# A gated attention and MLP kernel: the softmax shift from the first 512 keys, a half chunk of x loaded later, one split on GpSimd

## The chip, the core and the metric

The kernel runs on one core of a Trainium2 chip. The metric is the device time of one execution in microseconds (us). The core has five engines with a queue of instructions each, worked off in order: PE (matrix products, results in PSUM), DVE (vector), ACT (scalar functions, exponentials), POOL (GpSimd) and SP, which here only issues DMAs. Engines wait for each other by semaphores.

## The reference

One layer: `x` is 2048 x 512. Attention has 32 heads of 16 and one shared key and value head; beside it runs an MLP of width 1792 with squared ReLU; a gate per row mixes the two.

```python
g = sigmoid((x * gate_w).sum(-1, keepdims=True))
q = (x @ wq).reshape(B, S, 32, 16).transpose(0, 2, 1, 3)
k, v = x @ wk, x @ wv
p = softmax(einsum("bhqd,bkd->bhqk", q, k) * 16 ** -0.5)
a = einsum("bhqk,bkd->bhqd", p, v).transpose(...).reshape(B, S, 512) @ wo
b = maximum(x @ w1 + b1, 0) ** 2 @ w2 + b2
return g * a + (1 - g) * b
```

## The kernel before

Products in fp32 are made of rounded parts: each operand is split into `r` (rounded to a faster format) and `l` (the rest), and `r*r + r*l + l*r` is summed. So `xr`, `xl` stand for x, `wqr`, `wql` for wq, `qr`, `ql` for q; making a pair takes one cast and one subtraction.

The softmax uses no row maximum. Its shift is a bound: the norm of the query times the greatest norm of a key. The score product itself applies it: `qa` holds the rows of q and one row with the query norms (`nrm`), and `k_aug` holds the rows of k and one row with minus the greatest key norm (`km`), written by `k_shift`. A score group S is the product of 128 keys with 2 x 2 blocks of queries; ACT takes its exponential into a tile `e`; the context product (`acc<-e,v_ext`) sums `e` with v. At the end sums outside a safe range would send the kernel to an exact branch; this does not happen with these inputs.

The front, before the first score: x comes in four chunks of 512 rows, each in two DMAs of 512 KB (`x_load`; tiles `xf` for chunks 0 and 1, `xk` for 2 and 3), wq in four blocks (`wq_load`, tiles `wqf`). `kv_sums` makes k and v of one chunk, `kv_copy` copies them to SBUF (`kvc`), `k_rows` spreads k over the rows that `k_aug` needs, `k_round` (ACT) and `k_parts` (DVE) put it there. `kv_gather`, `kv_keep` and `kv_turn` turn k and v so that keys stand on partitions: for the key norms (`k_squares`, then the maximum) and for `v_ext`. `q_early` makes the first block of q, `qnorm` its norms, `q_direct` brings them into `qa` by SP's and POOL's DMA queues.

After that the work is interleaved. A span is one unit of other work (a block of q, of the MLP, of a projection): a number of matrix products M into one PSUM bank named `mm`, of which there are two, so the third unit takes the bank of the first. A phase is one text such as `"S0 M K M S1 ..."`: S is a score group, M a product of the unit, `02` and `12` the two halves of a score group that DVE copies from a third bank (`x`) into `e`, and K in the first phase a step left over from the front. While the program is written out, a planner keeps the estimated times of PE, ACT and DVE and places DVE's and ACT's other work by a list (`soon`: the span from which an entry may go, its cost, the work), in its order: the first entry has to go before the second is looked at. `wq_round` rounds a block of wq on ACT, `wq_rest` subtracts on DVE. When a unit of q is done, DVE casts its bank into `qr` and forms `ql` and the squares; with that the bank is free.

Nothing reorders instructions on the chip: the order on each engine is the order in which the program writes them out.

Of the kernel before, what the change touches and what calls it, by code (L numbers as in the profile page):

```python
# [58 lines left out]
    (4, 4, SECOND): ("02 S0 M M S1 M 12 M S3", (0, 1, 3, 2)),  # L59
    (4, 3, WHOLE): ("M 02 S0 M S1 12 M S3", (0, 1, 3, 2)),  # L60
}
FIRST_PHASE = "S0 M K M S1 M M M 02 M S3 M M M S4 M 12 M M S5", (0, 1, 3, 4, 5, 2)
HC = CH // 2

Q_ROWS = (0, 0, DH), (DH, 0, DH), (RS + 1, 1, DH), (RS, 2, 1)
FRONT_A, FRONT_V = 8, 22
LAST_OK = NC * KT - 1
FULL = 128 * LW * NC * KT

# [104 lines left out]
def mix_kernel(ctx: ExitStack, tc: tile.TileContext, xT, xs, gw, wkv, wq, wo, w12, b1, b2, cst, out):  # L174
# [67 lines left out]
    with fast, tc.tile_pool(name="at", bufs=1) as at, \  # L242
# [8 lines left out]
        def aside():  # L251
            return mp.tile([128, CH], F32, name="x", bufs=1)
# [8 lines left out]
        nc.scalar.dma_start(wkvf, wkv)  # L261
        xf, xw = {}, {}

        def x_load(c):

            for a in range(2):
                xw[c, a] = (at.tile([128, 2, CH], F32, name="xf", tag="e", bufs=10) if c < 2 else
                            at.tile([128, 2, CH], F32, name="xk", tag="w2p", bufs=5))
                nc.sync.dma_start(xw[c, a], xT[c, a])  # L269
            for k in range(KT):  # L270
                xf[c, k] = xw[c, k // 2][:, k % 2]

        def wq_load(t, n):
            nc.sync.dma_start(wqp[t // 2][:, t % 2:t % 2 + n], wq[t:t + n].rearrange("t p m -> p t m"))
# [1 line left out]
        x_load(0)  # L276
        wq_load(0, 1)
        nc.sync.dma_start(cs, cst)
        for c in range(1, NC):
            x_load(c)  # L280
        wq_load(1, 1)
        nc.gpsimd.dma_start(b1t, b1)
        gwb = at.tile([128, D], F32, name="gwb", tag="lc", bufs=2)

        blk = at.tile([128, 32], BF, name="blk")
        ones = at.tile([96, 128], BF, name="ones")
        kmx = at.tile([128, NK], F32, name="kmx")
        kmt = at.tile([128, 1], F32, name="kmt")
        km = at.tile([128, 1], F32, name="km")
        z = at.tile([128, NS], F32, name="z")  # L290
# [5 lines left out]
        for i in range(FRONT_V):  # L296
# [1 line left out]


        ks = {}  # L300
        rows_of = {0: lambda: two[:, 0], 1: lambda: late_kv[:, 1], 2: aside,
                   3: lambda: mp.tile([128, CH], F32, name="mm")}
        kvt = [at.tile([128, 2, CH], F32, name="kvc", tag="e", bufs=10) for _ in range(2)]
        kvc = [t[:, i] for t in kvt for i in range(2)]
        kvq, kb = {}, {}
# [1 line left out]
        def kv_sums(c, parts=range(KT)):  # L307

            if parts[0] == 0:
                kvq[c] = late_kv[:, 0] if c == 3 else aside() if c == 1 else mp.tile([128, CH], F32, name="mm")  # L310
            for k in parts:
                nc.tensor.matmul(kvq[c][32 * k:32 * k + 32], wkvf[:, k], xf[c, k], start=True, stop=True,
                                 skip_group_check=True, tile_position=(0, 32 * k))

        def kv_copy(c):
            nc.scalar.activation(kvc[c], kvq[c], AF.Copy)
# [19 lines left out]
                else:  # L336
                    nc.vector.tensor_scalar(row, src, -1.0, None, op0=OP.mult)  # L337

        ks2 = []
        kvg, gathered = [], {}  # L340

        def kv_gather(c):

            gathered[c] = mp.tile([128, CH], F32, name="mm") if c % 2 else aside()
            for j in range(4):
                nc.tensor.matmul(gathered[c][32 * j:32 * j + 32, :128], cs[:, C_SEL:C_SEL + 2 * DH],
                                 kvc[c][:, j * 128:(j + 1) * 128], start=True, stop=True,
                                 skip_group_check=True, tile_position=(0, 32 * j))

        def kv_keep(c):  # L350
            if not kvg:
                kvg.append(of_tile("kvg", F32))
            nc.scalar.activation(kvg[0][:, c * 128:(c + 1) * 128], gathered[c][:, :128], AF.Copy)

        def kv_turn(c):
            nc.tensor.transpose(acc[:, c * 128:(c + 1) * 128], kvg[0][:, c * 128:(c + 1) * 128], ident)

        def k_squares(i, n):
            if not ks2:
                ks2.append(of_tile("ksq", F32)[:, :NK * DH].rearrange("p (i d) -> p i d", i=NK))  # L360
            ksq = ks2[0]
            k = kvp[:, i:i + n, :DH]
            nc.scalar.activation(ksq[:, i:i + n], k, AF.Square)
            nc.vector.tensor_reduce(kmx[:, i:i + n], ksq[:, i:i + n], AX.X, OP.add)

        def k_max():
            nc.vector.tensor_reduce(kmt, kmx, AX.X, OP.max)
            pn = mp.tile([128, CH], F32, name="mm")
            nc.tensor.matmul(pn[:, :128], kmt.to_broadcast([128, 128]), ident, start=True, stop=True)

            def rest():
                nc.vector.tensor_reduce(km, pn[:, :128], AX.X, OP.max)
                nc.vector.tensor_scalar(km.bitcast(I32), km.bitcast(I32), 0.5, ROOT, op0=OP.mult, op1=OP.add)

            return rest

        def v_rows():
            nc.vector.tensor_copy(v_ext[:, :, 0:32:2], kvp[:, :, DH:])
# [11 lines left out]
        def of_tile(name, dt=F32R):  # L390
            return at.tile([128, CH], dt, name=name, tag="of", bufs=10)
# [8 lines left out]
        def q_early():  # L400
            q = mp.tile([128, CH], F32, name="mm")
            mm(q, q_terms(0, 0))
            qr, ql = of_tile("qr"), of_tile("ql")

            def rest():
                nc.vector.tensor_tensor(ql, q, qr.bitcast(F32), OP.subtract)
                nc.vector.tensor_tensor(sq8[:, 0], qr.bitcast(F32), qr.bitcast(F32), OP.mult)

            return qr, ql, (lambda: nc.scalar.activation(qr, q, AF.Copy)), rest

# [25 lines left out]
        def qnorm(tiles, p8=None):  # L436

            if p8 is None:
                p8 = aside()
            n = 32 * len(tiles)  # L440
            for i, (it, sq) in enumerate(tiles):
                nc.tensor.matmul(p8[32 * i:32 * i + 32], blk, sq, start=True, stop=True, tile_position=(0, 32 * i))  # L442
            nrm, tmp = of_tile("nrm"), of_tile("tmp", F32)
            root(nrm[:n], p8[:n], tmp[:n])
            if tiles[0][0] == 0:
                q_direct(RS, nrm, 1, (nc.sync, nc.gpsimd))
            for i, (it, sq) in enumerate(tiles):
                nc.sync.dma_start(qs[2][it:it + 2].rearrange("u r d a n -> (u r d a) n"),
                                  nrm[32 * i:32 * i + 8].bitcast(F32))
                done.update((it, it + 1))  # L450
# [110 lines left out]
        def wq_round(t):  # L561
            nc.scalar.activation(wqr[:, t], wqf[t], AF.Copy)
# [35 lines left out]
        wq_round(0)  # L598
        wq_rest(0)
        kv_copy(0)  # L600
        nc.vector.tensor_copy(blk, cs[:, C_BLK:C_BLK + 32])
        qr, ql, q_round, q_rest = q_early()
        x_pair(1, 0)
        kv_sums(1)
        two = sp.tile([128, 2, CH], F32, name="s")
        k_rows(0)
        nc.scalar.activation(xr[1][:, 2:], xw[1, 1], AF.Copy)  # L607
        q_round()
        q_rest()
        q_direct(0, qr, DH, (nc.sync, nc.gpsimd))  # L610
        q_direct(DH, qr, DH, (nc.sync, nc.gpsimd))
        q_direct(RS + 1, ql, DH, (nc.sync, nc.gpsimd))
        wq_load(2, 2)
        kv_copy(1)
        kv_gather(0)
        k_round(0)
        kv_keep(0)
        k_parts(0)
        kv_sums(2)
        qnorm([(0, sq8[:, 0])], mp.tile([128, CH], F32, name="mm"))  # L620
        kv_copy(2)
        acc = ap.tile([128, CH], F32, name="acc")
        kvp = acc.rearrange("p (i d) -> p i d", i=NK)
        kv_turn(0)
        kv_gather(1)
        kv_keep(1)
        kv_gather(2)
        kv_keep(2)
        nc.vector.tensor_tensor(xl[1][:, 2:], xw[1, 1], xr[1][:, 2:].bitcast(F32), OP.subtract)
        late_kv = sp.tile([128, 2, CH], F32, name="s")  # L630
        kv_sums(3)
        kv_copy(3)
        kv_turn(1)
        kv_turn(2)
        k_squares(0, 12)
        kv_gather(3)
        kv_keep(3)
        kv_turn(3)
        k_squares(12, 4)
        wq_round(1)  # L640
        k_rows(1)
        norm = k_max()
        nc.vector.tensor_copy(wqr[:, 2], wqf[2])
        k_rows(2)
        k_round(1)
        norm()
        k_shift(0, True)
        k_parts(1)
        k_round(2)
        k_parts(2)  # L650
        wq_rest(1)
        q_write(0, 0, qr, ql, nc.sync)

        def last_rows():

# [5 lines left out]
            act(0.6)  # L661
            dve(0.75)

        held, begun = 0.0, [0]
        chores, divisions = [], []
        soon = [(1, 0.7, lambda: wq_rest(2)), (1, 0.9, lambda: k_shift(1)), (1, 0.4, v_rows),
                (1, 0.7, lambda: (act(0.64), wq_round(3), wq_rest(3))), (2, 0.9, lambda: k_shift(2)), (3, 0.9, lambda: k_shift(3)),
                (3, 0.0, lambda: gates())]
        soon += [(6, 1.2, lambda k=k: x_split(2, k)) for k in range(KT)]
# [628 lines left out]
        def phase(slots, n, m):  # L1298
# [23 lines left out]
            for i in range(len(rows[0])):  # L1322
                for r in range(2):
                    item = rows[r][i]
                    if item == "M":
                        span.product(r)
                    elif item == "K":
                        if r == 0:
                            last_rows()
                    elif item[0] == "S":  # L1330
                        score_part(scored + int(item[1:]), r)
                    else:
                        score_copy(scored + int(item[1:]), r)
                    exps(todo)
                at_pe += PAIR
# [164 lines left out]
```

## Time and profile before

| | before |
|---|---|
| median of 3 runs | 1173.19 us (1172.84 to 1173.22) |
| profiled execution | 1173.13 us |
| its span | 1171.6 us |
| PE busy | 1163.5 us (99%) |
| ACT busy | 1022.9 us (87%) |
| DVE busy | 687.2 us (59%) |
| POOL busy | 67.9 us (6%) |
| granted PE clock | 1.0 |

The profile is one execution. Its rows give the start and the length of an instruction in us, the engine, the line, what it writes and reads, and in brackets how long its engine sat idle before it and what ended that. `x8` counts instructions in a row; one fp32 product is two matmuls there, so four products are `x8`. A q behind an engine's name (`SPq`) is the queue that issues DMAs.

### The profile page before, as it was taken

How to read it: one execution, taken by the hardware profiler on the slowest of the kernel's cores; microseconds unless marked ns; L12 is line 12 of the kernel's file. 1: busy time of each engine (PE TensorE's matmuls, PEld its weight loads, DVE VectorE, ACT ScalarE, POOL GpSimd, SP SyncE). 2: the span in 40 equal slices, each digit the busy share in tenths (PEclk: the TensorE clock that was granted, in tenths of full speed). 3: DMA queues.
4: the chain of work that ended last, by engine and by line, in shares of the span. 5: the costliest groups of instructions: out<-in, count | busy, mean ns of one | idle time of the engine just before them, and what ended most of it. 6: DMA issues, size and time to landing. Idle time of an engine off the chain costs nothing.

```text
span 1171.6 us, 31973 instructions
## 1 busy us (share of the span) xinstructions
PE 1163.5 (99%) x13793; PEld 779.6 (67%) x13793; DVE 687.2 (59%) x1174; ACT 1022.9 (87%) x1143; POOL 67.9 (6%) x125
## 2 busy tenths in 40 slices
PE   8999999999999999999999999999999999999998
PEld 4666666676766666666666666666666666666665
DVE  6877886764754745553666636535556537534554
ACT  7789999999988888888888898989888888888885
POOL 1000111010100000100000000001000000001000
PEclk9999999999999999999999999999999999999999
DMA  7245535251533513320434305224215224222101
GB/s 265 98 157 174 185 110 199 92 195 48 174 121 119 181 39 119 110 83 20 145 110 141 97 20 176 98 66 154 65 47 168 79 66 133 95 75 92 56 38 39
DMA packets 49290, 130.26 MB, mean 111 GB/s; under 512 B 11350, under 2 KB 11846, under 8 KB 48632
## 3 DMA queue, kind: packets, MB, share of 16 engines
q1 hardware_dynamic: 37272, 90.68, 24.1%
q0 software_dynamic: 11728, 37.43, 8.8%
q8 instruction: 109, 1.79, 0.6%
q14 instruction: 37, 0.30, 0.1%
q10 hardware_dynamic: 144, 0.07, 0.0%
HBM read 87.92 MB, written 35.64 MB: 105 GB/s over the span
## 4 chain that ended last, share of the span: by engine, by line
PE 97%; DMA 1%; ACT 1%; SPq 0%; DVE 0%; issue 0%
PE acc L964 39%; PE mm L1271 34%; PE s L907 19%; PE x L907 5%; DMA xf<-in_xT 1%; DMA wqf<-in_wq 0%; ACT e L944 0%; DVE ot L1231 0%; SPq L414 0%; PE s L213 0%; SPq L269 0%; ACT xr L607 0%; PE mm L321 0%; PE x L1053 0%; PE x L442 0%
## 5 line engine op out<-in xcount | busy, mean ns | idle before, releaser
L944 ACT ACTIVATE e<-s 128x1024 f32<-128x1024 f32 x765 | 748.1, 1024 | 102.5 <-PE s L907 99.4
L928 DVE COPY e<-x 128x512 f32<-128x512 f32 x518 | 358.4, 692 | 444.8 <-PE x L907 276.0
L964 PE MATMUL acc<-e,v_ext 128*32 128x256 f32 x8192 | 470.2, 381 | 0.0
L907 PE MATMUL s<-qa,k_aug 49*128 49x512 f32 x1530 | 407.4, 410 | 0.5 <-DVE k_aug L337 0.3
L964 PEld LDWEIGHTS acc<-e,v_ext 128*32 128x32 f32 x8192 | 252.5, 110 | 192.7 <-issue 40.4
L944 ACT ACTIVATE e<-e 128x1024 f32<-128x1024 f32 x259 | 272.8, 1056 | 0.2 <-ACT e L944 0.2
L907 PEld LDWEIGHTS s<-qa,k_aug 49*128 49x128 f32 x1530 | 214.7, 185 | 85.4 <-ACT e L944 38.6
L1271 PE MATMUL mm<-w2p,hr 64*128 64x512 f32 x1128 | 242.2, 392 | 0.0
L907 PE MATMUL x<-qa,k_aug 49*128 49x512 f32 x518 | 213.7, 413 | 0.0
L1271 PEld LDWEIGHTS mm<-w2p,hr 64*128 64x128 f32 x1128 | 160.8, 186 | 18.8
L1271 PE MATMUL mm<-xragain,w1p 64*128 64x512 f32 x448 | 119.7, 392 | 0.0
L907 PEld LDWEIGHTS x<-qa,k_aug 49*128 49x128 f32 x518 | 95.3, 184 | 36.1 <-DVE e L928 19.1
L1271 PE MATMUL mm<-xr,w1p 64*128 64x512 f32 x448 | 114.7, 392 | 0.0
L1271 PEld LDWEIGHTS mm<-xragain,w1p 64*128 64x128 f32 x448 | 70.0, 186 | 6.9
L1271 PEld LDWEIGHTS mm<-xr,w1p 64*128 64x128 f32 x448 | 68.9, 186 | 5.9
L1271 PE MATMUL mm<-xlagain,w1p 64*128 64x512 f32 x224 | 69.6, 396 | 0.0
L1271 PE MATMUL mm<-xl,w1p 64*128 64x512 f32 x224 | 66.5, 393 | 0.0
L1271 PE MATMUL mm<-more 64*128 64x512 f32 x216 | 60.4, 394 | 0.0
L1018 ACT ACTIVATE accs<-acc 128x256 f32<-128x256 f32 x60 | 23.1, 384 | 28.7 <-PE acc L964 26.9
L790 DVE TENSOR_SCALAR big<-mm,b1t 128x512 f32<-128x512 f32 x56 | 41.6, 742 | 0.0
L791 DVE TENSOR_TENSOR big<-big 128x512 f32<-128x512 f32 x56 | 38.8, 692 | 1.9
L1271 PEld LDWEIGHTS mm<-xlagain,w1p 64*128 64x128 f32 x224 | 35.7, 186 | 4.1
(197 smaller groups left out, 805.5 us busy)
## 6 DMA issues: line engine op xcount, KB each, us to landing
w1p<-w1kept SPq DMA_DIRECT2D x42, 512.0 KB
w2p<-w2kept SPq DMA_DIRECT2D x35, 512.0 KB
qa<-qs SPq DMA_DIRECT2D x186, 64.0 KB
w1kept<-w1p POOLq DMA_DIRECT2D x14, 512.0 KB, 3.6
w2kept<-w2p POOLq DMA_DIRECT2D x12, 512.0 KB, 5.1
qs<-qr SPq DMA_DIRECT2D x16, 256.0 KB
ress<-res POOLq DMA_DIRECT2D x4, 1024.0 KB, 5.5
qs<-ql POOLq DMA_DIRECT2D x15, 256.0 KB, 3.8
```

Source lines behind the costliest of these rows:

```text
L790: nc.vector.tensor_scalar(h[0], p, b1t[:, f:f + 1], 0.0, op0=OP.add, op1=OP.max)
L791: nc.vector.tensor_tensor(h[0], h[0], h[0], OP.mult)
L907: nc.tensor.matmul(dst.rearrange("p (a n) -> p a n", a=2), k_aug[rows, kt * 128:(kt + 1) * 128], qa[it][rows, :, q * HC:q * HC + HC], star ...
L928: nc.vector.tensor_copy(e_half(u)[:, 2 * r:2 * r + 2], x.rearrange("p (a n) -> p a n", a=2))
L944: nc.scalar.activation(e_half(u), src, AF.Exp, scale=SCALE)
L964: nc.tensor.matmul(accs[q][h * 32:(h + 1) * 32], v_ext[:, kt], es[u][:, h % 2 * 2 + h // 2], start=kt == 0 and it > 0, stop=kt == NK - 1, ...
L1018: nc.scalar.activation(a[:, q * HC:q * HC + HC], acc, AF.Copy)
L1271: nc.tensor.matmul((self.before if r else self).bank, a[p], b[p], start=not r and i == 0, stop=r == 1 and i == len(self.terms[1]) - 1, ski ...
```

## The change

It has these parts, all of them in the front:

- The key norm of the shift is taken over the first 512 keys (chunk 0) alone. `k_squares` and the maximum work on four columns in place of sixteen, and the gathering and turning of chunks 1 to 3 is left for v, as two K steps of the first phase (`v_gather`, `v_turn`). `v_rows` is put at the head of `soon` for span 2.
- Of the last chunk of x, the second half is loaded behind the query norms, as are the last two blocks of wq. The half of the sums that needs it becomes the first K step (`last_sums`); the last row product is the second.
- The rest of the second half of chunk 1 (`xl`) is formed by GpSimd in place of DVE.
- `q_early` forms the squares before `ql`; ACT gets five, DVE one more small filler instruction; the second block of wq is rounded by DVE instead of ACT, the third one's cast goes into `soon`; the order of the front is rewritten.

```diff
-FIRST_PHASE = "S0 M K M S1 M M M 02 M S3 M M M S4 M 12 M M S5", (0, 1, 3, 4, 5, 2)
+FIRST_PHASE = "S0 M M K S1 M M M 02 M S3 M K M M S4 M K 12 M M K S5", (0, 1, 3, 4, 5, 2)
-FRONT_A, FRONT_V = 8, 22
+FRONT_A, FRONT_V = 8, 23
...
-        for c in range(1, NC):
-            x_load(c)
+        x_load(1)
+        x_load(2)
+        x_load(3, (0,))
         wq_load(1, 1)
...
-        def kv_keep(c):
-            if not kvg:
-                kvg.append(of_tile("kvg", F32))
-            nc.scalar.activation(kvg[0][:, c * 128:(c + 1) * 128], gathered[c][:, :128], AF.Copy)
+        def kv_keep(c, n, copy):
+            copy(kvg[:, c * 128:(c + n) * 128], acc[:, c * 128:(c + n) * 128])
...
+        def k_squares():
+            nc.scalar.activation(ksq, kvp[:, :4, :DH], AF.Square)
+
+        def k_top():
+            nc.vector.tensor_reduce(kmx, ksq, AX.X, OP.add)
             nc.vector.tensor_reduce(kmt, kmx, AX.X, OP.max)
...
             def rest():
+                nc.vector.tensor_tensor(sq8[:, 0], qr.bitcast(F32), qr.bitcast(F32), OP.mult)
                 nc.vector.tensor_tensor(ql, q, qr.bitcast(F32), OP.subtract)
-                nc.vector.tensor_tensor(sq8[:, 0], qr.bitcast(F32), qr.bitcast(F32), OP.mult)
...
                 q_direct(RS, nrm, 1, (nc.sync, nc.gpsimd))
+                x_load(3, (1,))
+                wq_load(2, 2)
...
         kv_copy(0)
+        for i in range(FRONT_A // 2 + 1):
+            nc.scalar.activation(front[:, :1], wu[:, :1], AF.Copy)
         nc.vector.tensor_copy(blk, cs[:, C_BLK:C_BLK + 32])
         qr, ql, q_round, q_rest = q_early()
         x_pair(1, 0)
-        kv_sums(1)
...
         k_rows(0)
+        kv_gather(0)
         nc.scalar.activation(xr[1][:, 2:], xw[1, 1], AF.Copy)
         q_round()
         q_rest()
...
-        wq_load(2, 2)
...
+        kv_keep(0, 1, scalar_copy)
+        k_round(0)
+        kv_sums(1)
+        kv_turn(0)
+        ksq = kvg[:, CH - 4 * DH:].rearrange("p (i d) -> p i d", i=4)
+        k_squares()
+        qnorm([(0, sq8[:, 0])])
+        nc.gpsimd.tensor_tensor(xl[1][:, 2:], xw[1, 1], xr[1][:, 2:].bitcast(F32), OP.subtract)
+        k_top()
         kv_copy(1)
+        kv_sums(2)
+        kv_copy(2)
+        late_kv = sp.tile([128, 2, CH], F32, name="s")
+        k_rows(1)
+        k_parts(0)
+        pn = k_norm()
+        k_root(pn)
+        k_round(1)
+        k_shift(0, True)
+        k_rows(2)
+        k_round(2)
+        late_ks = mp.tile([128, CH], F32, name="mm")
+        kv_sums(3, (0, 1))
+        nc.vector.tensor_copy(wqr[:, 1], wqf[1])
+        wq_rest(1)
         k_parts(1)
...
+        def last_sums():
+
+            kv_sums(3, (2, 3))
+            kv_copy(3)
...
+        def v_gather():
+
+            for c in range(1, NC):
+                kv_gather(c)
+            kv_keep(1, 3, scalar_copy)
+
+        def v_turn():
+
+            for c in range(1, NC):
+                kv_turn(c)
+            soon.insert(0, (2, 0.4, v_rows))
+
+        aside_steps = [last_sums, last_rows, v_gather, v_turn]
...
-        soon = [(1, 0.7, lambda: wq_rest(2)), (1, 0.9, lambda: k_shift(1)), (1, 0.4, v_rows),
+        soon = [(1, 0.7, lambda: (nc.vector.tensor_copy(wqr[:, 2], wqf[2]), wq_rest(2))),
+                (1, 0.9, lambda: k_shift(1)),
                 (1, 0.7, lambda: (act(0.64), wq_round(3), wq_rest(3))), (2, 0.9, lambda: k_shift(2)), (3, 0.9, lambda: k_shift(3)),
                 (3, 0.0, lambda: gates())]
...
-                            last_rows()
+                            aside_steps.pop(0)()
```

What the change moves, at three places. First ACT, from the rows of chunk 2 (`kb<-x`) through the first phase and the one behind it, before:

```order
L325 ACTIVATE kb<-x 128x512
L944 ACTIVATE e<-s 128x1024
L325 ACTIVATE kb<-mm 128x512
L944 ACTIVATE e<-s 128x1024 x4
L944 ACTIVATE e<-e 128x1024
L562 ACTIVATE wqr<-wqf 128x512
L944 ACTIVATE e<-s 128x1024 x9
```

and after:

```order
L316 ACTIVATE kvc<-mm 128x512
L950 ACTIVATE e<-s 128x1024 x2
L325 ACTIVATE kb<-mm 128x512
L950 ACTIVATE e<-s 128x1024
L539 ACTIVATE kvg<-acc 128x384
L950 ACTIVATE e<-s 128x1024
L950 ACTIVATE e<-e 128x1024
L950 ACTIVATE e<-s 128x1024 x4
L555 ACTIVATE wqr<-wqf 128x512
L950 ACTIVATE e<-s 128x1024 x5
```

The exponentials are S0, S1, S3, S4, S5, then S2 (`e<-e`), then S6 to S9 of the second phase (the first S0 stands ahead of the rows of after). The copies `kvc` and `kvg` now stand among them, and the rounding of the last block of wq (`wqr<-wqf`) stands behind S9 in place of behind S2: `v_rows`, which may go from span 2 on, is now ahead of it in `soon`.

On DVE, behind the first phase, after (`peek` is DVE's one-element read that marks the end of a bank's products):

```order
L934 COPY e<-x 128x512
L1401 COPY peek<-mm 128x1
L369 COPY v_ext<-acc 128x256
L558 TENSOR_TENSOR wql<-wqf,wqr 128x512
L337 TENSOR_SCALAR k_aug<-km 1x512 x4
L205 CAST xr_88<-xk 128x512
L206 TENSOR_TENSOR xl_92<-xk,xr_88 128x512
L414 CAST qr<-mm 128x512
L415 TENSOR_TENSOR ql<-mm,qr 128x512
```

Here nothing moved, the kernel before has the same rows in the same order: `wql`, which reads what ACT rounds, stands ahead of the cast of the first unit's bank (`qr<-mm`, `ql`). From here to the end the order on all engines is that of the kernel before.

SP's queue, behind the first loads of x, before:

```order
L269 DMA xk<-in_xT 128x1024 x4
L274 DMA wqf<-in_wq 128x512
L414 DMA qa<-qr 16x2x512 x2
L414 DMA qa<-ql 16x2x512
L274 DMA wqf<-in_wq 128x2x512
L414 DMA qa<-nrm 1x2x512
```

and after:

```order
L269 DMA xk<-in_xT 128x1024 x3
L274 DMA wqf<-in_wq 128x512
L405 DMA qa<-qr 16x2x512 x2
L405 DMA qa<-ql 16x2x512
L405 DMA qa<-nrm 1x2x512
L269 DMA xk<-in_xT 128x1024
L274 DMA wqf<-in_wq 128x2x512
```

One half chunk of x moved from the fourth place of its row to behind the norms, and the two blocks of wq moved behind it.

More of the change, by code (lines that the diff above doesn't have):

```diff
@@ L262, in mix_kernel, with x_load @@
         xf, xw = {}, {}
-        def x_load(c):
-            for a in range(2):
+        def x_load(c, parts=range(2)):
+            for a in parts:
                 xw[c, a] = (at.tile([128, 2, CH], F32, name="xf", tag="e", bufs=10) if c < 2 else
@@ L269, in x_load @@
                 nc.sync.dma_start(xw[c, a], xT[c, a])
-            for k in range(KT):
-                xf[c, k] = xw[c, k // 2][:, k % 2]
+                for k in (2 * a, 2 * a + 1):
+                    xf[c, k] = xw[c, a][:, k % 2]
         def wq_load(t, n):
@@ L286, in mix_kernel @@
         ones = at.tile([96, 128], BF, name="ones")
-        kmx = at.tile([128, NK], F32, name="kmx")
+        kmx = at.tile([128, 4], F32, name="kmx")
         kmt = at.tile([128, 1], F32, name="kmt")
@@ L300, in mix_kernel @@
         ks = {}
-        rows_of = {0: lambda: two[:, 0], 1: lambda: late_kv[:, 1], 2: aside,
-                   3: lambda: mp.tile([128, CH], F32, name="mm")}
+        rows_of = {0: lambda: two[:, 0], 1: lambda: late_kv[:, 0], 2: aside, 3: lambda: late_ks}
         kvt = [at.tile([128, 2, CH], F32, name="kvc", tag="e", bufs=10) for _ in range(2)]
@@ L309, in kv_sums @@
             if parts[0] == 0:
-                kvq[c] = late_kv[:, 0] if c == 3 else aside() if c == 1 else mp.tile([128, CH], F32, name="mm")
+                kvq[c] = late_ks if c == 3 else mp.tile([128, CH], F32, name="mm")
             for k in parts:
@@ L337, in k_shift @@
                     nc.vector.tensor_scalar(row, src, -1.0, None, op0=OP.mult)
-        ks2 = []
-        kvg, gathered = [], {}
         def kv_gather(c):
-            gathered[c] = mp.tile([128, CH], F32, name="mm") if c % 2 else aside()
             for j in range(4):
-                nc.tensor.matmul(gathered[c][32 * j:32 * j + 32, :128], cs[:, C_SEL:C_SEL + 2 * DH],
+                nc.tensor.matmul(acc[32 * j:32 * j + 32, c * 128:(c + 1) * 128], cs[:, C_SEL:C_SEL + 2 * DH],
                                  kvc[c][:, j * 128:(j + 1) * 128], start=True, stop=True,
@@ L348, in kv_gather @@
                                  skip_group_check=True, tile_position=(0, 32 * j))
-        def kv_keep(c):
-            if not kvg:
-                kvg.append(of_tile("kvg", F32))
-            nc.scalar.activation(kvg[0][:, c * 128:(c + 1) * 128], gathered[c][:, :128], AF.Copy)
+        def kv_keep(c, n, copy):
+            copy(kvg[:, c * 128:(c + n) * 128], acc[:, c * 128:(c + n) * 128])
         def kv_turn(c):
-            nc.tensor.transpose(acc[:, c * 128:(c + 1) * 128], kvg[0][:, c * 128:(c + 1) * 128], ident)
@@ L358, in k_squares @@
[L358 to L366, printed above, removed]
-            nc.vector.tensor_reduce(kmt, kmx, AX.X, OP.max)
[L368 to L375, printed above, removed]
+            nc.tensor.transpose(acc[:, c * 128:(c + 1) * 128], kvg[:, c * 128:(c + 1) * 128], ident)
@@ new lines, in k_squares, with k_norm, k_root @@
+        def k_squares():
+            nc.scalar.activation(ksq, kvp[:, :4, :DH], AF.Square)
+        def k_top():
+            nc.vector.tensor_reduce(kmx, ksq, AX.X, OP.add)
+            nc.vector.tensor_reduce(kmt, kmx, AX.X, OP.max)
+        def k_norm():
+            pn = acc[:, CH - 128:]
+            nc.tensor.matmul(pn, kmt.to_broadcast([128, 128]), ident, start=True, stop=True)
+            return pn
+        def k_root(pn):
+            nc.vector.tensor_reduce(km, pn, AX.X, OP.max)
+            nc.vector.tensor_scalar(km.bitcast(I32), km.bitcast(I32), 0.5, ROOT, op0=OP.mult, op1=OP.add)
@@ L603, in mix_kernel @@
         x_pair(1, 0)
-        kv_sums(1)
         two = sp.tile([128, 2, CH], F32, name="s")
+        kvg = of_tile("kvg", F32)
+        acc = ap.tile([128, CH], F32, name="acc")
+        kvp = acc.rearrange("p (i d) -> p i d", i=NK)
         k_rows(0)
+        kv_gather(0)
         nc.scalar.activation(xr[1][:, 2:], xw[1, 1], AF.Copy)
@@ L612, in mix_kernel @@
         q_direct(RS + 1, ql, DH, (nc.sync, nc.gpsimd))
-        wq_load(2, 2)
+        kv_keep(0, 1, scalar_copy)
[7 more added lines that the diff above has]
+        k_top()
         kv_copy(1)
-        kv_gather(0)
-        k_round(0)
-        kv_keep(0)
+        kv_sums(2)
+        kv_copy(2)
+        late_kv = sp.tile([128, 2, CH], F32, name="s")
+        k_rows(1)
         k_parts(0)
[L619 to L643, printed above, removed]
-        k_rows(2)
-        k_round(1)
-        norm()
-        k_shift(0, True)
+        pn = k_norm()
+        k_root(pn)
+        k_round(1)
+        k_shift(0, True)
+        k_rows(2)
+        k_round(2)
[3 more added lines that the diff above has]
+        wq_rest(1)
         k_parts(1)
-        k_round(2)
         k_parts(2)
-        wq_rest(1)
         q_write(0, 0, qr, ql, nc.sync)
+        def last_sums():
+            kv_sums(3, (2, 3))
+            kv_copy(3)
         def last_rows():
```

## The prediction, made before the changed kernel was run

> **What bounds the kernel now.** I read the page, then the execution cut into three windows, then the chain of waits of the first 40 us, since the change touches nothing later.
>
> ```profile
> span 1171.6 us, 31973 instructions
> 20.79:34.60 13.81, 13.38 (x109) 8.35 (x109) 11.18 (x21) 11.53 (x14) 0.15 (x1) 1.00 0.29 90
> 34.60:1171.60 1137.00, 1132.67 (x13591) 764.37 (x13587) 663.30 (x1111) 997.41 (x1101) 64.78 (x116) 1.00 0.33 108
> ```
>
> Columns of the last two: window, its length, then the busy time of PE, weight loads, DVE, ACT, POOL. After 34.6 us PE is busy for 1132.67 of 1137.00 us. Whatever delays or advances PE's work at 34.6 us therefore reaches the end of the kernel undiminished, and only the front has to be worked out. Its chain:
>
> ```profile
> 13.81 5.63 DMA wqf<-in_wq
> 19.46 0.43 DVE wqr L643
> 20.31 0.43 DVE k_aug L337
> 20.79 0.70 PE s L907 x2
> ...
> 31.91 2.73 PE acc L964 x48
> 34.63 0.43 PE mm L1271 x2
> ```
>
> The first score (S0) starts at 20.79, behind the load of the last two blocks of wq (landed at 19.44), a cast, and the shift. The first context (P·V) runs from 31.91 to 34.63; then PE begins the third unit of q (`mm L1271`). That unit has a second condition:
>
> ```profile
> PEld mm L1271 <- DVE ql L424: 0.4, 1, 0.4
> 28.59 0.61 ACT L562 ACTIVATE wqr<-wqf 128x512 fp32r<-128x512 f32 x1
> 29.23 0.69 DVE L565 TENSOR_TENSOR wql<-wqf,wqr 128x512 fp32r<-128x512 f32 x1 [2.05 <-ACT wqr L562]
> 29.94 1.72 DVE L337 TENSOR_SCALAR k_aug<-km 1x512 fp32r<-1x512 f32 x4
> 33.46 0.69 DVE L424 TENSOR_TENSOR ql<-mm,qr 128x512 fp32r<-128x512 f32 x1
> 34.56 0.50 PE L1271 MATMUL mm<-xr,wqr 64*128 64x512 f32 x2
> ```
>
> The third unit writes the PSUM bank that the first unit of the interleaved phase filled, so it waits until DVE has cast that bank and formed its `ql`. DVE works in order: first `wql` of the last block of wq (which waited 2.05 us for ACT's rounding at 28.59), four shift rows, one cast and subtraction of x, the cast of q, and `ql`, which ends at 34.15. From the start of `wql` to the end of `ql` are 34.15 - 29.23 = 4.92 us without a pause that counts. The bank is free 0.4 us before PE needs it (34.56). This 0.4 us is all the slack there is, and the argument below is about it.
>
> **The change, part by part.**
>
> *Ahead of S0: about 2 us gained.* Rows of the work that moves there:
>
> ```profile
> 2.77 1.84 ACT L295 ACTIVATE front<-wu 128x1 f32<-128x1 bf16 x8
> 8.91 1.06 ACT L587 ACTIVATE xr<-xf 128x1024 fp32r<-128x1024 f32 x1 [0.62 <-DMA xf<-in_xT]
> 12.38 0.68 DVE L407 TENSOR_TENSOR sq<-qr 128x512 bf16<-128x512 f32 x1
> 15.07 0.41 DVE L383 CAST nrm<-tmp 32x512 fp32r<-32x512 f32 x1
> 10.79 1.07 PE L312 MATMUL x<-xf,wkvf 128*32 128x512 f32 x8
> 15.08 0.40 PE L346 MATMUL x<-kvc,cs 128*32 128x128 f32 x8
> 16.41 0.44 PE L356 MATMUL acc<-cs,kvg 128*128 128x128 f32 x2
> 18.17 1.02 PE L321 MATMUL s<-kvc,cs 128*128 128x512 f32 x2
> ```
>
> Five more one-element copies on ACT are 5 x 0.23 = 1.15 us. They follow the copy of the first sums, end near 9.45, and push the rounding of x from 8.91; of this some 0.2 us reach `qr`, since ACT idled for a chunk after that. The 23rd memset on DVE (0.12 us) lies in DVE's wait for the first x. Squares before `ql` bring the norms 0.6 us forward, and on PE one row product (1.02), one gather (0.25), one set of sums (1.04) and one turn (0.17) stand ahead of the norms' product: I get `nrm` ready at 14.9 instead of 15.48. The shift needs 64 key columns instead of 256: sums of chunk 2 end at 14.5, rows of chunk 1 at 15.6, the maximum's product 0.3 to 0.46 later, two small DVE steps, and the shift row stands at about 17.3. The second row product and half of the sums of chunk 3 end on PE at 17.6. The cast of wqr no longer stands ahead of the shift. The query norms reach `qa` through POOL's queue:
>
> ```profile
> qa<-nrm POOLq DMA_DIRECT2D x1, 4.0 KB, 3.9
> DMA to landing us min/median/max: 2.2/4.1/5.1
> ```
>
> (The second row is that of `ql`, the fastest and slowest of this queue here.) From 15.0 that is 17.2 to 18.9. So S0 comes at 17.6 to 18.9.
>
> *The half chunk of x, loaded behind the norms: most of it is given back.*
>
> ```profile
> 3.91 2.65 SPq L269 DMA_DIRECT2D xk<-in_xT  x4
> 15.52 0.71 SPq L414 DMA_DIRECT2D qa<-nrm  x1
> 1.09 0.87 SPq L269 DMA_DIRECT2D xf<-in_xT  x2
> 4.92 1.06 ACT L587 ACTIVATE xr<-xf 128x1024 fp32r<-128x1024 f32 x1 [0.30 <-DMA xf<-in_xT]
> ```
>
> Its issue moves from the last of the four at 3.91 to 6.56 to behind the norms' issue: 14.95 + 0.71 + 0.1 = 15.75. A load of 512 KB took 3.8 us on an empty queue (issued 1.09, used at 4.92) and 5.63 on a full one (wqf above). The queue ahead is now a half chunk and two blocks of wq shorter, so I take 4.15, near the empty one: landed at 19.9, bounds 19.55 and 21.4. S0 and two products of the unit run, then PE stands at the second half of the sums of chunk 3 until 19.9. They take half of 1.04, so S1 starts near 20.45. In the kernel before:
>
> ```profile
> 22.50 0.72 PE L907 MATMUL s<-qa,k_aug 49*128 49x512 f32 x2
> 25.73 0.50 PE L907 MATMUL s<-qa,k_aug 49*128 49x512 f32 x1
> 21.44 1.13 PE L321 MATMUL mm<-kvc,cs 128*128 128x512 f32 x2
> 24.65 2.95 ACT L944 ACTIVATE e<-s 128x1024 f32<-128x1024 f32 x3 [0.36 <-PE s L907]
> 27.62 1.06 ACT L944 ACTIVATE e<-e 128x1024 f32<-128x1024 f32 x1
> ```
>
> S1 is still 2.05 us ahead of 22.50. From S1 to S5 PE took 25.73 - 22.50 = 3.23. Now the last row product (1.05), which stood ahead of S1 at 21.44, stands behind it, and three gathers (0.72), three turns (0.5) and the wait for ACT's copy between them (0.1, an estimate: the copy is about 0.5 and PE has 0.69 of products) come on top: S5 starts 5.6 after S1, its exponential 0.6 later, at 26.65. Before it started at 24.65 + 2 x 0.97 = 26.6. The gain is used up.
>
> *ACT's rounding of the last block of wq: the term that decides.* Before, it stood right behind the exponential of the copied scores (27.62), at 28.59. Now four further exponentials (S6 to S9) stand ahead of it. From S5's exponential that is six of them: at 0.99 each (24.65 to 27.62) 5.94, at the 0.92 of undisturbed stretches 5.5; I take 5.7. The rounding starts at 32.35, DVE's `wql` 0.64 later (28.59 to 29.23) at 33.0, `ql` ends 4.92 later at 37.9. The queue of DVE behind `wql` is the same as before. PE ends the first context at about 34.4 and now waits for the bank until 37.95, where before it went on at 34.56: **+3.4 us**.
>
> In one line: landing + 0.55 + 6.2 + 5.7 + 0.64 + 4.92 + 0.05 - 34.56 = landing - 16.5. At 19.9 it is +3.4; at 21.4, with exponentials of 0.99, +5.1. Below, S0 on PE's earliest time (17.6) puts S1 at 18.9 however early the load is, and with 0.92 the sum is +1.65. No value in these bounds is a gain.
>
> *GpSimd forms the rest of x's second chunk.* On DVE this took:
>
> ```profile
> 15.42 1.21 DVE L629 TENSOR_TENSOR xl<-xf,xr 128x1024 fp32r<-128x1024 f32 x1
> ```
>
> The profile has no arithmetic of POOL, so its price is open: from below, the 1.21 of DVE; from above, the 15 us until something needs it (the buffer of x is reused by the exponential of S7 at about 29.5; the product itself is used by the fourth unit, after 38). I cost it at nothing, because nothing waits in that time; behind it on POOL stands only the next write of `ql`, at 34.45 before. DVE is 1.21 us lighter there, which shows only as an earlier shift. The first `wqr` cast and `wql` that move behind the shift, and the third block's pair that waits for its load at about 21, lie on DVE ahead of S2's copy and behind no score; `v_ext` is needed only at the context.
>
> [...]
>
> **Sum.** Profiled run 1173.13 (span 1171.6 and 1.5 around it), 0.06 below the median of 1173.19. With +3.4: **1176.6 us**. Two kernels nearer than 0.2% (2.35 us) can hardly be told apart here.
>
> **The rivals.**
>
> *The bank is free in time.* If DVE's chain did not hold the third unit, the end would be set by the phase itself. By the terms above the context would start 0.3 us earlier (0.5 us of rounding gone ahead of S6, against 0.05 at S5): 1172.9; with every early bound (S5's exponential at 25.1) 2 us: 1171.1. It decides if ACT's rounding starts before 28.95. For it: the 0.4 us shows that the bank was free before. Against it: six exponentials of 0.92 would have to begin by 23.4, which needs S1 before 17.2, ahead of even the earliest S0.
>
> *The load lands early.* A fixed cost of 2.2 us, as the fastest row of POOL's queue, would land it at 18; the early bound holds: +1.65 to +2.3, 1174.8 to 1175.5, no measurable change. [...]
>
> *GpSimd stops DVE at the shift.* If DVE's shift rows stood still until POOL's subtraction (from 15.6) has ended, S0 would come half a us after that end. S1 would then be later than I say from an end at 19.5 on, us for us. An end at 24, some half of the 15 us that bound it, gives S0 at 24.5, S1 at 26, and everything 5.5 us later than I say: about 1182. Against it: POOL's own rows here are short, and no row stands against DVE. [...]
>
> **How the numbers follow.** My case (landing 18.9 to 21.4): 0.67. Early load: 0.14. GpSimd's stop: 0.07. Bank free: 0.12, of which 0.08 within 0.2% and 0.04 better than its early bound. So slower 0.74, same 0.22, faster 0.04. The range takes my case and the early load (0.81): +1.65 to +5.1, 1174.8 to 1178.3, and 0.2 us on either side for the spread of the runs.
>
> **What the profile after would show.** S0 at 17.6 to 18.9; PE idle up to 20 waiting for `xk`, S1 at 20 to 21; S5's exponential at 26 to 27; ACT's `wqr` at 32 to 33; DVE idle for 5 us ahead of that `wql`; PE idle for 3 us or more from about 34.5, released by `ql`; POOL's subtraction over well before 29. I am wrong if ACT's `wqr` starts before 29, if PE goes on at 34.5 without a wait, or if a later stage gives time back.

## Result and profile after

| | before | after |
|---|---|---|
| median of 5 runs on one chip | 1173.11 us (1172.84 to 1173.22) | 1179.54 us (1179.35 to 1180.80) |
| ratio | | 1.0056, 95% interval 1.0044 to 1.0067 |
| profiled execution, span | 1173.13, 1171.6 us | 1180.80, 1179.2 us |

The change costs 6.4 us, where 3.4 were forecast. The profiled execution is the longest of the five; the other four lie between 1179.35 and 1179.59. Its mean granted clock is 0.997, theirs are 0.998 or 0.999; the last section comes back to this gap of 1.3 us.

The instructions on which the prediction's steps stand, from the trace after (start, length, engine, line, output and inputs; in brackets the idle time ahead and its releaser):

```profile
15.57 2.37 POOL L618 TENSOR_TENSOR xl<-xf,xr 128x1024 fp32r<-128x1024 f32 x1
16.18 2.05 DVE L337 TENSOR_SCALAR k_aug<-km 1x512 fp32r<-1x512 f32 x1
18.28 0.68 PE L913 MATMUL s<-qa,k_aug 49*128 49x512 f32 x2 [0.81 <-DVE k_aug L337]
20.45 0.50 PE L913 MATMUL s<-qa,k_aug 49*128 49x512 f32 x2
26.72 0.50 PE L913 MATMUL s<-qa,k_aug 49*128 49x512 f32 x2
27.26 1.03 ACT L950 ACTIVATE e<-s 128x1024 f32<-128x1024 f32 x1 [1.07 <-PE s L913]
29.28 3.75 ACT L950 ACTIVATE e<-s 128x1024 f32<-128x1024 f32 x4
32.89 0.65 ACT L555 ACTIVATE wqr<-wqf 128x512 fp32r<-128x512 f32 x1
33.57 0.69 DVE L558 TENSOR_TENSOR wql<-wqf,wqr 128x512 fp32r<-128x512 f32 x1 [6.25 <-ACT wqr L555]
37.82 0.69 DVE L415 TENSOR_TENSOR ql<-mm,qr 128x512 fp32r<-128x512 f32 x1
32.00 2.80 PE L970 MATMUL acc<-e,v_ext 128*32 128x256 f32 x48
38.66 0.79 PE L1277 MATMUL mm<-xr,wqr 64*128 64x512 f32 x2 [3.86 <-DVE ql L415]
41.39 1.02 PE L1277 MATMUL mm<-xr,wqr 64*128 64x512 f32 x2
45.78 2.80 PE L970 MATMUL acc<-e,v_ext 128*32 128x256 f32 x48
```

S0 is at 18.28, S1 at 20.45, S5 at 26.72. ACT's rounding of wq's last block stands behind the four exponentials of S6 to S9 and starts at 32.89. `wql` waits 6.25 us for it, `ql` ends at 38.51, and PE, done with the first context at 34.80, waits 3.86 us for the bank. It starts the third unit at 38.66 where the kernel before started it at 34.56: **+4.1 us**.

The second context starts at 45.78. In the kernel before it started at 39.01:

```profile
39.01 2.80 PE L964 MATMUL acc<-e,v_ext 128*32 128x256 f32 x48
```

So another 2.7 us were lost in between, in a stretch where PE never waits. The windows of this stretch show why. Columns: window, length, busy time of PE, weight loads, DVE, ACT, POOL with counts, then the granted clock of PE, DMA share and GB/s.

```profile
34.40:37.60 3.20, 0.40 (x8) 0.00 (x0) 3.10 (x7) 0.00 (x0) 0.00 (x0) 1.00 0.00 0
37.60:38.00 0.40, 0.00 (x0) 0.00 (x0) 0.37 (x2) 0.00 (x0) 0.00 (x0) 0.81 0.00 0
38.00:44.40 6.40, 5.74 (x28) 4.91 (x30) 4.80 (x9) 2.61 (x3) 0.76 (x1) 0.50 0.46 147
44.40:44.80 0.40, 0.40 (x6) 0.37 (x4) 0.00 (x0) 0.35 (x1) 0.00 (x0) 0.66 0.00 0
44.80:48.00 3.20, 3.20 (x54) 1.91 (x54) 2.76 (x5) 2.83 (x3) 0.48 (x1) 1.00 0.19 73
```

From about 37.9 to 44.7 the granted clock is 0.50. In the 6.40 us from 38.0 PE is busy for 5.74 with 28 matmuls, and in the 3.2 us from 44.8 it does 54. Successive pairs stand 0.43 us apart (the row at 41.39 is one of them) instead of 0.23. From 45.78 on nothing is given back. One of ACT's copies of a finished context, early and late in the program, before and then after:

```profile
87.04 0.38 ACT L1018 ACTIVATE accs<-acc 128x256 f32<-128x256 f32 x1 [0.72 <-PE acc L964]
1095.29 0.39 ACT L1018 ACTIVATE accs<-acc 128x256 f32<-128x256 f32 x1 [0.49 <-PE acc L964]
```

```profile
93.92 0.38 ACT L1024 ACTIVATE accs<-acc 128x256 f32<-128x256 f32 x1 [0.72 <-PE acc L970]
1102.87 0.38 ACT L1024 ACTIVATE accs<-acc 128x256 f32<-128x256 f32 x1 [0.51 <-PE acc L970]
```

The distance is 6.88 us early and 7.58 late. So the 7.6 us between the two spans are 4.1 of wait, 2.7 of half clock, and 0.8 in small parts behind it, 0.7 of them between these two copies. What the small parts are stays open.

### The profile page after: what moved, and what is told of

It is laid out like the page before. It is cut to its first block, busy times and chain, and to the rows that moved or that the text cites. A ratio compares the mean times of both kernels' runs of the same rounds, so it can differ in the third digit from the quotient of the medians.

```text
span 1179.2 us, 31979 instructions
## 1 busy us (share of the span) xinstructions
PE 1168.3 (99%) x13793; PEld 782.9 (66%) x13793; DVE 687.8 (58%) x1174; ACT 1023.5 (87%) x1144; POOL 70.5 (6%) x126
## 4 chain that ended last, share of the span: by engine, by line
PE 98%; DVE 1%; ACT 1%; DMA 0%; issue 0%; SPq 0%
PE acc L970 39%; PE mm L1277 34%; PE s L913 19%; PE x L913 5%; ACT e L950 0%; DMA xf<-in_xT 0%; DVE k_aug L337 0%; PE mm L213 0%; PE mm L312 0%; DVE ot L1237 0%; PE s L321 0%; PE s L213 0%; PE x L433 0%; PE acc L342 0%; ACT xr L580 0%
## 5 line engine op out<-in xcount | busy, mean ns | idle before, releaser
L1277 PEld LDWEIGHTS mm<-w2p,hr 64*128 64x128 f32 x1128 | 160.7, 186 | 18.5
L1277 PE MATMUL mm<-wor,orr 64*128 64x512 f32 x120 | 38.4, 394 | 0.0
```

The costliest lines, as they stand in the source:

```text
L1277: nc.tensor.matmul((self.before if r else self).bank, a[p], b[p], start=not r and i == 0, stop=r == 1 and i == len(self.terms[1]) - 1, ski ...
```

## The experiments

Theory A: ACT's rounding of wq's last block, moved behind four exponentials, makes PE wait for the bank, and this wait lets the clock drop. Rival B: the slow products come from what runs beside them (loads, DVE), not from the wait. Rival C: the front itself, with its late load and GpSimd holding DVE up, costs the time. All ratios and differences below are against runs of the kernel before on the same chip, 1173.01 to 1173.11 us.

**The order alone, in the kernel before.**

```diff
-        soon = [..., (1, 0.4, v_rows),
+        soon = [..., (2, 0.4, v_rows),
```

> The kernel before, with nothing changed but that v_rows may go from span 2 on instead of span 1; ACT's rounding of wq's last block then stands behind S9's exponential as in the changed kernel. Front, loads and GpSimd are those of before. Theory A: the rounding starts 4 exponentials later, near 32.3; PE goes on near 38.0 instead of 34.56, idle for 3.5 us; if that is long enough for the clock to drop (it dropped 3.2 us after PE went idle in the changed kernel) another 2.5 us: 1178.5 to 1179.5, and 1176.5 if the clock stays. Rival B: 1176.5, with the products at full pace. Rival C (the front costs it): 1173.0 to 1173.5, no change.

Measured: 1179.51 us (1178.34 to 1180.18), ratio 1.0054 (1.0040 to 1.0068). The profiled execution took 1178.58.

```profile
28.48 3.79 ACT L944 ACTIVATE e<-s 128x1024 f32<-128x1024 f32 x4
32.15 0.64 ACT L562 ACTIVATE wqr<-wqf 128x512 fp32r<-128x512 f32 x1
32.83 0.69 DVE L565 TENSOR_TENSOR wql<-wqf,wqr 128x512 fp32r<-128x512 f32 x1 [5.82 <-ACT wqr L562]
37.89 0.50 PE L1271 MATMUL mm<-xr,wqr 64*128 64x512 f32 x2 [3.84 <-DVE ql L424]
38.40:41.60 3.20, 3.20 (x17) 2.97 (x17) 3.10 (x7) 1.94 (x2) 0.40 (x1) 0.50 0.57 183
```

One number in one tuple gives the kernel before, with its old front, its loads and no GpSimd arithmetic, a loss of the same size as the change: 1179.51 against 1179.54. That the two medians agree so closely is partly luck: the five runs spread over 1.8 us, and the third unit starts 0.77 us earlier than in the changed kernel (37.89 against 38.66). The rounding starts at 32.15 in place of 28.59, PE waits 3.84 us, and the clock is at 0.50 behind it (last row, a window). Rival C falls as the main cause.

**The order back, in the changed kernel.**

```diff
-            soon.insert(0, (2, 0.4, v_rows))
+            soon.insert(0, (1, 0.4, v_rows))
```

> The changed kernel with v_rows entered at the head of `soon` for span 1 in place of span 2, so that ACT's rounding of wq's last block stands ahead of the exponentials of S6 to S9 again; the front with its late load and the GpSimd step stays as changed. Theory A (the place of that rounding makes PE wait for the bank, and the wait lets the clock drop): ACT's `wqr` starts 3.7 us (four exponentials) earlier, near 29.2 instead of 32.89; PE goes on with the third unit near 35 with less than 0.5 us of idle time, no stretch of half clock behind it, 1173.0 to 1173.9. Rival B (the slow products from 38.7 to 44.2 come from what runs beside them, the idle time being only 4.1 of the loss): the products of that stretch stay 0.43 us apart, 1175.4 to 1176. Rival C (the front, with GpSimd stopping DVE, costs it): still 1179 to 1180.

Measured: 1175.93 us (1175.69 to 1176.17), ratio 1.0024 (1.0015 to 1.0033).

```profile
29.33 0.61 ACT L555 ACTIVATE wqr<-wqf 128x512 fp32r<-128x512 f32 x1
29.98 0.69 DVE L558 TENSOR_TENSOR wql<-wqf,wqr 128x512 fp32r<-128x512 f32 x1 [2.60 <-ACT wqr L555]
33.51 0.42 DVE L205 CAST xr<-xk 128x512 fp32r<-128x512 f32 x1
35.29 0.69 DVE L415 TENSOR_TENSOR ql<-mm,qr 128x512 fp32r<-128x512 f32 x1
36.03 0.50 PE L1277 MATMUL mm<-xr,wqr 64*128 64x512 f32 x2 [0.66 <-DVE ql L415]
```

3.6 of the 6.4 us come back, and the clock stays at 1.00. But PE still reaches the third unit at 36.03, 1.47 later than before, against my "less than 0.5 us of idle time" near 35. Two things make it: the rounding starts at 29.33, 0.74 later than before, and the planner put a second pair of x (the cast at 33.51 and its subtraction, 1.06 us) ahead of `qr`. `ql` ends 1.83 later than before, of which the 0.4 of slack takes its part. The time lies above Theory A's 1173.0 to 1173.9 and inside Rival B's 1175.4 to 1176; but Rival B had it by products 0.43 us apart, and here they are 0.23 apart. So the order explains 3.6 us of the loss in this kernel, and it does not explain the other 2.8.

**The wait filled.** Products of zeros on PE behind the first context, in the changed kernel, read by nothing:

```diff
             context(range(u, u + m))
+            if u == 0:
+                d = aside()
+                for _ in range(16):
+                    nc.tensor.matmul(d, wu[:, :128], wu, start=True, stop=True)
```

> The changed kernel with 16 additional products of zeros (bf16, 128x512, nothing reads them) on PE right behind the first context, some 3.5 us of work at 0.22 each in the 3.9 us in which PE waits for `ql`. Theory A: the wait for the bank is the same (third unit near 38.7), but the granted clock stays at 1.0 and the products behind it are 0.23 us apart; the second context starts 2.5 to 2.8 us earlier than 45.8; 1176.7 to 1177.2. Rival B (the pace comes from the loads and the DVE work beside the products): no gain, 1179.3 to 1179.9, products 0.43 apart.

Measured: 1178.02 us (1177.81 to 1178.17), ratio 1.0041 (1.0027 to 1.0055).

```profile
34.78 3.63 PE L1417 MATMUL x<-wu 128*128 128x512 bf16 x16
38.71 0.50 PE L1277 MATMUL mm<-xr,wqr 64*128 64x512 f32 x2 [0.30 <-DVE ql L415]
34.40:48.00 13.60, 13.30 (x129) 8.70 (x120) 13.19 (x25) 6.74 (x8) 1.51 (x2) 1.00 0.31 108
```

The third unit starts where it did (38.71), beside the same loads and DVE work, but the clock is 1.00 throughout, and the second context starts at 43.10 instead of 45.78. Useless work in the wait makes the kernel 1.5 us faster. Rival B falls: the pace follows from the wait. The expectation of 1176.7 to 1177.2 took the 2.7 us of the profiled execution off the median; against the profiled 1180.80 they fit (1178.1). The other runs, which have no trace, would then have lost about 1.5 to half clock.

**How short a wait is harmless: 5 and 10 such products.**

> The changed kernel with 5 (not 16) additional products of zeros on PE behind the first context, so that PE's idle time ahead of the third unit shrinks from 3.9 us to about 2.8 and nothing else moves. In the runs so far the clock fell between 3.2 and 5.1 us after PE went idle, always after an idle time of 3.9, and stayed at half for 3.4 us or 6.6. Theory A1 (it takes an idle time longer than some 3.3 us, the length of one such stretch): the clock stays at 1.0 throughout, the third unit starts near 38.7, 1177.6 to 1178.4, the runs within 0.4 of each other as with 16 products. Rival A2 (any idle time of 2 to 3 us is enough, or the loads beside it bring it on): half clock again for 3 us or more, 1179 to 1180.5 with runs over 1 us apart.

> The changed kernel with 10 additional products of zeros on PE behind the first context (5 and 16 ran before). With 5 of them an idle time of 2.7 us was left ahead of the third unit and the clock still fell in the profiled run; with 16 an idle time of 0.3 was left and it did not. With 10 the idle time is about 1.6 us. If what counts is how much of a stretch of some 3.4 us PE sits idle, and half is the bound (A3), the clock stays: 1177.8 to 1178.2, the runs within 0.4 of each other, products 0.23 apart behind 38.7. If an idle time of 1.6 us is enough (A4): half clock for 3.4 us, 1179.2 to 1179.7 in most runs.

With 5: 1179.41 us, of five runs four at 1179.28 to 1179.64 and one at 1178.06. With 10: 1178.11 (1177.92 to 1178.29). Rows with 5, and behind them with 10:

```profile
38.69 0.50 PE L1277 MATMUL mm<-xr,wqr 64*128 64x512 f32 x2 [2.67 <-DVE ql L415]
38.80:39.20 0.40, 0.40 (x4) 0.39 (x6) 0.40 (x2) 0.00 (x0) 0.36 (x1) 1.00 0.98 369
39.60:42.40 2.80, 2.80 (x16) 2.64 (x14) 2.73 (x6) 1.94 (x2) 0.00 (x0) 0.50 0.61 195
42.80:46.00 3.20, 3.20 (x45) 2.24 (x46) 2.06 (x5) 2.92 (x4) 0.00 (x0) 1.00 0.02 6
```

```profile
38.80 0.50 PE L1277 MATMUL mm<-xr,wqr 64*128 64x512 f32 x2 [1.60 <-DVE ql L415]
38.80:44.00 5.20, 5.20 (x52) 4.37 (x56) 5.10 (x10) 4.17 (x5) 0.76 (x1) 1.00 0.57 181
```

A1 fell: in the trace a wait of 2.67 us is enough, and by their times it was in four of the five runs. One of 1.60 is not in the trace, and the times of all five runs say the same. The drop with 5 products comes at about 39.3, when PE is already busy again, and lasts until 42.75.

**GpSimd's part undone.** The subtraction on DVE, behind `k_parts(2)`, in the changed kernel:

```diff
-        nc.gpsimd.tensor_tensor(xl[1][:, 2:], xw[1, 1], xr[1][:, 2:].bitcast(F32), OP.subtract)
...
         k_parts(2)
+        nc.vector.tensor_tensor(xl[1][:, 2:], xw[1, 1], xr[1][:, 2:].bitcast(F32), OP.subtract)
```

> The changed kernel with the rest of x's second chunk formed on DVE (1.21 us there) behind the two `k_parts`, GpSimd free of it. Theory A: DVE's shift row takes 0.4 us in place of 2.05, S0 comes near 17.3 instead of 18.28; S1 follows the load and comes between 19.0 and 20.0 instead of 20.45; the chain behind S1 and the context move alike, so PE's idle time and the half clock stay: 1178.1 to 1179.2. If the load and not the shift set S1: 1179.5, no change. Rival C (the front costs all of it): 1173 to 1174.

Measured: 1180.28 us (1179.96 to 1181.23), ratio 1.0062 (1.0048 to 1.0075).

```profile
16.13 0.42 DVE L337 TENSOR_SCALAR k_aug<-km 1x512 fp32r<-1x512 f32 x1
17.35 0.50 PE L913 MATMUL s<-qa,k_aug 49*128 49x512 f32 x2
19.26 1.05 PE L312 MATMUL mm<-xk,wkvf 128*32 128x512 f32 x4 [0.94 <-DMA xk<-in_xT]
20.24 0.51 PE L913 MATMUL s<-qa,k_aug 49*128 49x512 f32 x2
38.45 0.50 PE L1277 MATMUL mm<-xr,wqr 64*128 64x512 f32 x2 [3.86 <-DVE ql L415]
```

The shift row takes 0.42 us again instead of 2.05, and S0 comes 0.93 us earlier. But now PE waits for the half chunk of x, which lands at 19.26, and S1 gains 0.21. The wait for the bank is 3.86 as before. GpSimd's hold on DVE is real and costs the third unit only these 0.2 us; the load stood right behind it. The time missed both forecasts (1178.1 to 1179.2, and 1179.5), and the median is 0.7 above the changed kernel's. In the traces the second context starts 1.4 us earlier (44.39), and yet the profiled execution is only 0.5 shorter (1180.28 against 1180.80). The rest is lost in later small parts, which stay open.

**What is left when the wait is taken away.** The changed kernel with v_rows for span 1 and wq's last block rounded by DVE, not ACT:

```diff
-                (1, 0.7, lambda: (act(0.64), wq_round(3), wq_rest(3))), ...
+                (1, 0.7, lambda: (nc.vector.tensor_copy(wqr[:, 3], wqf[3]), wq_rest(3))), ...
```

> The changed kernel with v_rows in `soon` for span 1, and wq's last block rounded by DVE (0.43 us, where DVE sat idle for 2.6 us) in place of ACT; late load and GpSimd step as changed. Theory A (what is left in the run with v_rows for span 1, +2.8, comes from that rounding still standing on ACT ahead of S6, 0.7 us later than before, and from one more pair of x ahead of `qr`): `wql` starts near 27.8, `qr` by 32.5, PE goes on right behind the first context near 34.8, +0.2 against before; 1173.2 to 1174.4 (up to 1.2 us come later in small parts in every run of the changed front). Rival C (the front itself costs 2 to 3 us): 1175.5 to 1176.5.

Measured: 1175.04 us (1174.77 to 1175.22), ratio 1.0016 (1.0007 to 1.0025).

```profile
27.90 0.69 DVE L558 TENSOR_TENSOR wql<-wqf,wqr 128x512 fp32r<-128x512 f32 x1
32.17 0.69 DVE L415 TENSOR_TENSOR ql<-mm,qr 128x512 fp32r<-128x512 f32 x1
34.82 0.50 PE L1277 MATMUL mm<-xr,wqr 64*128 64x512 f32 x2
```

PE goes on at 34.82, without a wait, +0.26 against before, as Theory A had it. Still the kernel is 2.0 us slower, above the 1174.4 that I had allowed and below Rival C's 1175.5. In the trace the distance to before is 0.61 us at 64 us and 1.55 at 1095 us. The same one edit in the kernel before:

> The kernel before with one thing changed: wq's last block is rounded by DVE instead of ACT. Theory A: ACT is 0.6 us lighter ahead of S6, PE's wait of 0.22 at S8 goes, the first context starts 0.2 to 0.5 us earlier and the third unit follows it at once: 1172.5 to 1173.1. A rival: DVE's cast delays nothing but gains nothing, 1173.1.

Measured: 1173.59 us (1173.27 to 1174.47), ratio 1.0005 (0.9996 to 1.0014), no difference that can be told. Its third unit starts 0.14 earlier than before (I had put 0.2 to 0.5), and by 1095 us its profiled execution is 0.93 behind. So such small later losses come without the changed front too; what they are stays open.

**The load at two other places.** Both kernels have DVE's subtraction, v_rows for span 1 and DVE's rounding; in the first the half chunk of x is loaded with the rest of x, in the second between `ql` and the norms.

```diff
-        x_load(3, (0,))
+        x_load(3)
...
-                x_load(3, (1,))
```

> The changed kernel with the rest of x's second chunk on DVE, v_rows for span 1, wq's last block rounded by DVE, and the last half chunk of x loaded with the rest of x as before instead of behind the query norms. Theory A: without the wait for that load the sums of it run right behind S0's products, S1 near 19.2 instead of 20.45, S5 near 25.5; ACT's exponentials lead to the context near 31.0, third unit near 33.8; 1171.8 to 1173.0 with the small later parts. Rival D (the half load then holds up the query norms, which come by the same queue): S0 later than 18.5, and no gain over the kernel with the late load.

> As the kernel with the rest of x's second chunk on DVE, v_rows for span 1 and wq's last block rounded by DVE, but the last half chunk of x is loaded between the last rows of `ql` and the query norms (neither with the rest of x as before nor behind the norms). In the profile of the changed kernel little is moved between 14.5 and 17.5 us (20 to 180 GB/s in place of 400), so the load would fall into a hole: issued near 14.0, landed by 17.8. Theory A (S1's place sets the end, 1 us for 1 us): norms landed by 17.5 and S0 17.4 to 18.0, S1 18.6 to 19.4 against 20.28 with the load ahead of all, context 30.3 to 31.2, 1173.0 to 1174.0. Rival D (the load holds the norms up as it did when it stood ahead of all): S0 at 18.3 or later, S1 as there, 1174.7.

Measured: with the rest of x 1174.68 us (1174.41 to 1175.70), ratio 1.0014 (1.0005 to 1.0023); between `ql` and the norms 1174.92 (1174.54 to 1175.38), 1.0014 (1.0005 to 1.0023). Rows of the first, then of the second, then of the kernel with the load behind the norms and GpSimd's part undone:

```profile
18.27 0.74 PE L912 MATMUL s<-qa,k_aug 49*128 49x512 f32 x2 [0.77 <-DMA qa<-nrm]
20.28 0.50 PE L912 MATMUL s<-qa,k_aug 49*128 49x512 f32 x2
qa<-nrm POOLq DMA_DIRECT2D x1, 4.0 KB, 3.2
```

```profile
20.67 0.50 PE L913 MATMUL s<-qa,k_aug 49*128 49x512 f32 x2
qa<-nrm POOLq DMA_DIRECT2D x1, 4.0 KB, 3.3
```

```profile
qa<-nrm POOLq DMA_DIRECT2D x1, 4.0 KB, 2.0
```

Rival D came, though the first kernel's S0, at 18.27, is ahead of the 18.5 that it named: with the load ahead of them the norms take 3.2 and 3.3 us to land instead of 2.0, and S0 waits for them (in the first the row says so; in the second, at 18.70, its row names an operation of DVE on other keys, and the norms' landing at 18.4 is the nearest that fits). S1 is at 20.28, 20.67 and 20.24: either the norms or the load is late, and their order decides nothing. None of these kernels beats the kernel before.

## Why the prediction was wrong

- *S0 at 17.6 to 18.9*: 18.28, but held there by GpSimd. Without it 17.35, a little ahead of my bound.
- *The load lands at 19.9, S1 0.55 later, at 20.45*: S1 came at 20.45 by two errors that cancel. The load lands at 19.26 (seen with GpSimd's part undone); the half set of sums behind it takes 0.98 us to S1, not 0.55; GpSimd adds 0.2. I had halved the 1.04 us of a whole set. The traces have a whole set as `x8` in 1.04 us before and each half as `x4` in 1.05, so splitting the set also cost PE a second 1 us.
- *S5's exponential 6.2 us behind S1*: 6.81. This is the term that was mis-sized. ACT idled 1.07 us for S5, so PE was late; the row product, gathers and turns, and the breaks between them, took more than I had put. It makes 0.6 of the 0.7 us by which the third unit came later than forecast.
- *5.7 us of exponentials, then 0.64, 4.92 and 0.05*: measured 5.63, 0.68, 4.94 and 0.15. The chain through ACT's rounding, `wql`, `ql` and the bank was right in every link, and the kernel before with only that order shows that this alone is enough for a loss of this size.
- *GpSimd costed at nothing*: nearly right in the sum (0.2 us at S1), wrong in the reason. The rival's wait is there (2.05 us for a row of 0.42), but POOL ended at 17.94, ahead of the 19.5 from which I had it decide.
- *The bank is free in time, the load early*: neither. ACT's rounding started 3.9 us behind the 28.95 that the first needed.
- **The step that failed**: "Whatever delays or advances PE's work at 34.6 us therefore reaches the end of the kernel undiminished" took PE's pace behind the wait for granted. A wait of 3.86 us put the third unit 4.1 us later, and then 1.5 or 2.7 more were lost, since PE went on at half clock. No term of the sum and no rival had it, and the range ended below it. With the wait filled, and so without the half clock, the same kernel took 1178.02, which lies inside the range. My list for the trace said PE would idle "for 3 us or more from about 34.5"; the two windows of before on which that step rests have a granted clock of 1.00 and no such wait with work behind it, so they could not show at what pace PE goes on.

The median run would add up as 4.1 (wait) + 1.5 (one stretch of half clock) + 0.8 (later parts) = 6.4; the 1.5 is from the traces of other kernels, as this kernel's only trace is that of its longest run. With the wait filled it is 4.1 + 0.8 = 4.9 (1178.02).

## What to carry to other kernels

Before a chore is moved behind other work on an engine, ask which engine's next step waits for it, and how much slack the trace shows there: here 0.4 us stood against 3.7. Where the answer is a new idle time of PE, look for a slower pace behind it too: here the wait cost 4.1 us and the half clock behind it 1.5 or 2.7 more, and filling the wait with 16 products that nothing reads took the median from 1179.54 to 1178.02 us. With a load that is put behind a small urgent transfer, ask whether what needs the load can wait too: here the norms landed in 2.0 us in place of 3.2, and PE then waited 0.94 us for the load.

## What the runs showed of the hardware

Ahead of the third unit the granted clock fell in the traces with an idle time of PE of 2.67 us (5 products), 3.84 (late rounding in the kernel before) and 3.86 (the changed kernel, and the one with DVE's subtraction), and in no trace with 1.60 or less. It did not fall at a fixed time: 3.1 us after the idle time began in the changed kernel, 3.3 with 5 products, 4.2 in the kernel before with the late rounding, 5.1 with DVE's subtraction; in the last three PE was busy again by then. Behind PE's last product the clock of the changed kernel fell at 1177.9, 1.7 us into the idle time; that of the kernel before stayed at 1.00 to the end of its span, 3.05 us into it. Worked out from windows of 0.40 us, it stayed at 0.50 ahead of the second context for 3.41 us in three traces and for 6.83 in the changed kernel's, twice as long, and the cost went with it: from the third unit to the second context 5.94 us in those three, 7.12 in the one, 4.45 before.

In the 3.41 us ahead of the drop PE had sat idle for 3.05 us (changed kernel), 3.02 (late rounding), 2.67 (5 products) and 2.17 (DVE's subtraction); with 10 products, where it did not drop, PE's wait at this place was 1.60. In the 3.41 us behind it PE was busy throughout in the three, and still idle for 0.81 in the changed kernel, where the clock stayed down for a second such time. These counts agree with A3, which put the bound at half of such a stretch (1.7 us), but four traces do not prove it, and the end of the kernel before, idle for 3.05 us without a drop, does not show it. What sets the moment of the drop and the length of 3.41 us was not shown.

Every run gives a mean granted clock beside its time. In the kernel before with the late rounding the two runs at 1178.34 and 1178.58 have a mean clock of 0.999, the three at 1179.51 to 1180.18 one of 0.996 or 0.997. The spread of the times alone says less: it is 1.3 to 1.8 us with the full wait and 0.4 with 10 or 16 products, but the kernel before has spread over 0.4 to 1.3 as well.

GpSimd's subtraction of 128x1024 took 2.37 us, DVE's 1.21. Beside it a DVE operation on one partition (`1x512`) took 2.05 us instead of 0.42 and ended at 18.23, 0.29 after GpSimd's. Two small DVE operations just ahead of it, from 15.66 and 15.99, took 0.29 and 0.15 us beside GpSimd, and 0.29 and 0.15 with GpSimd's part undone. Why the one was held and the two were not, no run here shows.
